# Positive and negative features of a head side by side: one pass for K^T V, 84-column matmuls for phi_q KV, and a new order

## The chip, the cores and the metric

The kernel runs on one core of one Trainium2 chip. TensorE (PE) multiplies matrices into PSUM; VectorE (DVE), ScalarE (ACT) and GpSimd (POOL) do the elementwise work and the sums; SyncE (SP) issues nearly all DMAs. The metric is the device time of one execution in microseconds. Before the change it is 297.68 us, the median of three runs from 297.18 to 297.76 us.

## The reference

One layer in bf16 with 2048 tokens of width D = 640: linear attention with learned feature maps on 32 heads of 20 dimensions, then a gated block without an activation function. Cut to what matters here:

```python
q, k, v = qkv of layernorm(x), heads of Dh = 20
pq = einsum("bhsd,hdf->bhsf", q, w_phi)          # and pk from k
phi_q = concat([softmax(pq), softmax(-pq)], -1)  # 40 features of a head
phi_k = concat([softmax(pk), softmax(-pk)], -1)
kv  = einsum("bhsf,bhsd->bhfd", phi_k, v)
z   = einsum("bhsf->bhf", phi_k)
num = einsum("bhqf,bhfd->bhqd", phi_q, kv)
den = einsum("bhqf,bhf->bhq", phi_q, z) + 1e-6
h   = x + (num / den) @ wo
out = h + ((ln(h) @ w_gate) * (ln(h) @ w_up)) @ w_down   # F = 1536
```

## The kernel before

Tokens are cut into NT = 16 tiles of P = 128 rows, D into NC = 5 chunks of 128. Features are 2 x 640 per token: the 640 positive ones of all heads (s = 0), then the 640 negative ones (s = 1). A chunk of 128 features of one sign touches 7 or 8 heads of 20 (the list CH, 36 heads over the five chunks).

Units, with the names that the order uses:

- `warm` is 48 matmuls on ones before data is there. `wk`, `x`, `y`, `wm`, `wv`, `c`, `wo` prepare weights (w_phi is multiplied into wq and wk; means are taken out). `s` computes layernorm's statistics of the rows; their inverse root goes into `rs` by a POOL instruction.
- `k`t (keys, L738): projection into PSUM, ten matmuls of 320 columns; then softexp (L725): DVE takes the largest absolute value (`mx`, L726) and multiplies it by `rs` (`nb`, L729, one column), ACT writes the two exponentials (L733). `K`t: DVE sums groups of 20 (L744) and takes reciprocals (L746), POOL multiplies all 1280 features by them in place (L747).
- `v`t: projection, ACT writes the values with a one behind each head's 20 (`vaug`, 21 columns a head, L753).
- `A`t and `B`t (kv_mm, L790): K^T V of a pair of tiles, for the positive (A) and the negative (B) features. A matmul has 128 features as weights and the 147 or 168 columns of the heads that they touch; each of A and B holds a PSUM buffer of two banks until `Aout` and `Bout` (kv_out, L812), where DVE multiplies by a mask (`Gkv`) that leaves only each feature's own head, and the epsilon is added to the column of sums. There are four such PSUM buffers (`PS`, pool p_ps) for everything.
- `q`t (queries, L758): projection and softexp as for keys, into one of three buffers `eq`; the positive half leaves at once by a DMA transpose into `phiqT`. `Q`t: DVE sums (L767), a ratio of the two sums of a head (L769, L770), POOL multiplies the negative half by it (L775), and a second DMA transpose takes that half.
- `n`t (num, L834): phi_q KV of a tile, twelve matmuls: two signs, five chunks, and the middle chunk in two parts since its heads lie in two PSUM banks. DVE divides (L862, L863), the result is transposed (on PE for the first two tiles, by DMA for the others).
- `h`t (watt): output projection, residual (L882), transpose into `hT`, statistics. `f`b.ft.j (fu): gate and up matmuls of a block of four tiles (in block 0 two tiles at a time), ACT copies the gate (L903), DVE multiplies (L905). `d`t and `e`t: down projection and the store.

Num of any tile needs K^T V of all sixteen. A block's `f` needs `h` of its tiles.

The order of every engine's queue is made by a planner in the kernel's text (`place`, L183) from the dictionary ORDER and the duration `t` and latency `lat` that each operation states. An engine's operations are sorted by the place of their unit in its list. At each step the planner looks at the first few of each queue that are left (AHEAD: 4 for PE and POOL, 6 for the others), takes of those whose inputs are already placed the one that can start first, and gives it its buffers; only if no engine has such an operation may it look further down the lists, and takes the first one that is ready. So a unit's place in the list is a preference, and what the queue becomes depends on the durations too. On the chip each engine runs its queue strictly in order and waits on semaphores.

Of the kernel before, what the change touches and what calls it, by code (L numbers as in the profile page):

```python
# [11 lines left out]
P = 128  # L12
# [17 lines left out]
NKV = 2 * sum(hi - lo + 1 for lo, hi in CH)  # L30

KVG = [[(0, 0), (1, 0), (2, 0)], [(3, 0), (4, 0)], [(0, 1), (1, 1), (2, 1)], [(3, 1), (4, 1)]]
# [28 lines left out]
    "DVE":  # L61
# [8 lines left out]
    "ACT":  # L70
# [8 lines left out]
    "POOL":  # L79
# [292 lines left out]
def _build(ctx, nc, A_x, A_wqkv, A_w_phi, A_wo, B_w_gate, B_w_up, B_w_down, out):  # L372
# [16 lines left out]
    phiqT = sb([P, 2, 2, NC, 512], BF16, "phiqT")  # L389
    KVsb = sb([P, E21 * NKV], BF16, "KVsb")  # L390
# [32 lines left out]
    phik = BK[:, :].rearrange("p (t s n) -> p t s n", t=NT, s=2)  # L423
    pq = phiqT[:, :, :, :, :].rearrange("p b s c n -> p (b s c n)")
# [30 lines left out]
    R_KV, R_Gkv = Reg(), regs(4)  # L455
# [87 lines left out]
    def act_sum(in_, func, acc, rd, wr):  # L543
        v = Buf(p_junk)
        g.op("ACT", lambda e: e.activation(out=junk[:, v.i, :], in_=in_, func=func, accum_out=acc),  # L545
             rd=rd, wr=wr, use=[v], t=0.93, lat=1.0)
# [16 lines left out]
    def stats(i0, n):  # L563
# [18 lines left out]
        g.op("DVE", lambda e: e.tensor_copy(sm[:, sl], PS[v.i][:, 1, 0:n]), rd=[v.R[1]], wr=R_sm[sl], use=[v], t=0.15, lat=0.2)  # L582
        if not act:
            v3 = Buf(p_t32)
            sq = lambda: t32[:, v3.i, 0:P * n].rearrange("p (t n) -> p t n", t=n)
            g.op("DVE", lambda e: e.tensor_tensor(out=sq(), in0=PS[v.i][:, 0, 0:P * n].rearrange("p (t n) -> p t n", t=n),
                                                  in1=ident[:, :].unsqueeze(1).to_broadcast([P, n, P]), op=ALU.mult),
                 rd=[v.R[0], R_id], wr=v3.R, use=[v, v3], t=0.09 + 0.15 * n, lat=0.2 + 0.15 * n)
            g.op("DVE", lambda e: e.tensor_reduce(out=sxx[:, sl], in_=sq(), axis=AX.X, op=ALU.add), rd=v3.R, wr=R_sxx[sl], use=[v3],
                 t=0.09 + 0.14 * n, lat=0.2 + 0.14 * n)  # L590
# [21 lines left out]
    def nmu_out(v, bk, w, eng):  # L612
        if eng == "ACT":
            g.op("ACT", lambda e: e.activation(out=nmu[:, w, :, :], in_=PS[v.i][:, bk, 0:NC].unsqueeze(2).to_broadcast([P, NC, P]),
                                               func=ACT.Copy, scale=-1.0 / SC), rd=[v.R[bk]], wr=[R_nmu[w]], use=[v], t=0.72, lat=0.8)
        else:
            g.op("DVE", lambda e: e.tensor_scalar(out=nmu[:, w, :, :], in0=PS[v.i][:, bk, 0:NC].unsqueeze(2).to_broadcast([P, NC, P]),  # L617
                                                  scalar1=-1.0 / SC, scalar2=None, op0=ALU.mult),
                 rd=[v.R[bk]], wr=[R_nmu[w]], use=[v], t=0.77, lat=0.85)
# [7 lines left out]
    def wk_in():  # L627
# [27 lines left out]
    def wp_round(w, i):  # L655
# [23 lines left out]
        if i % 2 == 0:  # L679
            g.op("ACT", lambda e: e.activation(out=dst, in_=PS[v.i][:, :, 0:HALF], func=ACT.Copy, scale=SC),  # L680
                 rd=v.R, wr=[R_Wp[w][i]], use=[v], t=0.62, lat=0.72)
        else:
            g.op("DVE", lambda e: e.tensor_scalar(out=dst, in0=PS[v.i][:, :, 0:HALF], scalar1=SC, scalar2=None, op0=ALU.mult),
                 rd=v.R, wr=[R_Wp[w][i]], use=[v], t=0.7, lat=0.8)
# [10 lines left out]
    def wv_centre(v, cs):  # L695
        for c in cs:
# [5 lines left out]
                 t=0.81, lat=0.9)  # L702


    def wo_mean(c):
# [4 lines left out]
             rd=[R_wsum[c]], app=[R_Wo[c]], t=0.2)  # L710
# [13 lines left out]

    def softexp(v, t, i, dst, regs_, use=()):  # L725
        g.op("DVE", lambda e: e.tensor_reduce(out=mx[:, i:i + 1], in_=PS[v.i][:, :, 0:HALF], axis=AX.XY, op=ALU.max,  # L726
                                              apply_absolute_value=True, negate=True), rd=v.R, wr=[R_mx[i]], use=[v],
             t=0.81, lat=0.9)
        g.op("DVE", lambda e: e.tensor_tensor(out=nb[:, i:i + 1], in0=mx[:, i:i + 1], in1=rs[:, t:t + 1], op=ALU.mult),  # L729
             rd=[R_mx[i], R_rs[t]], wr=[R_nb[i]], t=0.16, lat=0.2)  # L730
        for s in range(2):
            sc = rs if s == 0 else nrs
            g.op("ACT", lambda e, s=s, sc=sc: e.activation(  # L733
                out=dst(s).rearrange("p (b n) -> p b n", b=2), in_=PS[v.i][:, :, 0:HALF], func=ACT.Exp,
                bias=nb[:, i:i + 1], scale=sc[:, t:t + 1]), rd=v.R + [R_nb[i], R_rs[t], R_nrs[t]], wr=[regs_[s]], use=[v] + list(use),
                t=0.88, lat=0.96)

    def keys(t, after=()):  # L738
        U("k%d" % t)
        softexp(proj(t, 1, after), t, t, lambda s: phik[:, t, s, :], R_phik[t])  # L740
        U("K%d" % t)
        vs, vr = Buf(p_Ss), Buf(p_Rk)
        x = phik[:, t, :, :].rearrange("p s (h f) -> p (s h) f", f=DH)
        g.op("DVE", lambda e: e.tensor_reduce(out=Ssum[:, vs.i, :], in_=x, axis=AX.X, op=ALU.add), rd=R_phik[t], wr=vs.R, use=[vs],  # L744
             t=1.5, lat=1.52)
        g.op("DVE", lambda e: e.reciprocal(out=Rk[:, vr.i, :], in_=Ssum[:, vs.i, :]), rd=vs.R, wr=vr.R, use=[vs, vr], t=0.55, lat=0.62)  # L746
        g.op("POOL", lambda e: e.tensor_tensor(out=x, in0=x, in1=Rk[:, vr.i, :].unsqueeze(2).to_broadcast([P, 2 * H, DH]), op=ALU.mult),  # L747
             rd=vr.R + R_phik[t], wr=R_phik[t], use=[vr], t=2.36)

    def values(t):  # L750
# [5 lines left out]
             rd=v.R + [R_rs[t]], app=[R_vaug[t]], use=[v], t=0.8, lat=0.88)  # L756

    def queries(t, after=()):  # L758
# [8 lines left out]
        g.op("DVE", lambda e: e.tensor_reduce(out=Sq[:, vs.i, :], in_=eq[:, b.i, :, :].rearrange("p s (h f) -> p (s h) f", f=DH),  # L767
                                              axis=AX.X, op=ALU.add), rd=b.R, wr=vs.R, use=[b, vs], t=1.5, lat=1.52)
        g.op("DVE", lambda e: e.reciprocal(out=rq[:, vr.i, :], in_=Sq[:, vs.i, H:2 * H]), rd=vs.R, wr=vr.R, use=[vs, vr], t=0.38, lat=0.38)  # L769
# [222 lines left out]
    for t in range(0, NT, 2):  # L992
        kv_mm(0, t, t + 2)
# [53 lines left out]
```

## Time and profile before

| | |
|---|---|
| median of the runs (3) | 297.68 us |
| lowest, highest | 297.18, 297.76 us |
| span of the profiled execution, first to last instruction | 296.0 us |
| granted TensorE clock | 1.000 of full speed |
| matmuls; LDWEIGHTS | 2375; 2389 |
| K^T V matmuls of 147 and of 168 columns | 128 and 32 |
| num matmuls of 147 and of 84 columns | 128 and 64 |
| DVE `mx` x32, `nb` x32, mean of one | 810 ns, 386 ns |
| DVE sums of keys L744 x16, of queries L767 x16 | 1461 ns, 1476 ns |
| ACT exponentials, 640 elements, x64 | 883 ns |
| POOL L747 (keys) x16, L775 (queries) x16 | 2356 ns, 1269 ns |
| DMA transposes phiqT<-eq x32, issue to landing | 2.6 us |

The profile names an instruction by the line of the kernel that issues it; all matmuls in the main loops go through one helper, L552, and are told apart by what they write and read. Buffers share memory, so some names mislead: the gate's results are written into the space of `phik`, w_down into that of `vaug`. A matmul's duration holds its way through the array; the next one starts long before it ends.

### The profile page before, as it was taken

The numbers are of one execution on the slowest core, as the hardware profiler recorded it, in microseconds if no ns is written. First come the engines' busy times: TensorE is split into PE (matmuls) and PEld (weight loads), VectorE is DVE, ScalarE is ACT, GpSimd is POOL, SyncE is SP. The second block draws the span as 40 slices with busy tenths as digits, with TensorE's granted clock in tenths as the row PEclk, the third lists the DMA queues.
The fourth block names the chain that finished last, engine by engine and source line by source line (L and its number), as shares of the span: only waits on it lengthen the run. The fifth ranks groups of instructions, "written<-read, shape, count | busy, mean of one in ns | idle before, by whom it ended". The sixth has DMA issues, their size and how long they took to land.

```text
span 296.0 us, 5789 instructions
## 1 busy us (share of the span) xinstructions
PE 288.0 (97%) x2375; PEld 201.1 (68%) x2389; DVE 182.0 (61%) x314; ACT 136.3 (46%) x226; POOL 104.0 (35%) x140
## 2 busy tenths in 40 slices
PE   8999999999998999999999999999999999999996
PEld 8878767886876888878665666567645444654673
DVE  1799999999999888978768584431132224023122
ACT  1447878977747555615416323341343313332121
POOL 7428977869521332231500324123132000230010
PEclk9999999999999999999999999999999999999999
DMA  8998899301459543444622354331111000010012
GB/s 202 195 201 132 205 354 395 127 2 39 52 114 264 112 90 71 80 87 79 122 35 62 75 90 108 72 66 47 44 47 23 21 0 2 22 44 2 0 44 69
DMA packets 65194, 28.10 MB, mean 95 GB/s; under 512 B 55696, under 2 KB 63888, under 8 KB 65168
## 3 DMA queue, kind: packets, MB, share of 16 engines
q1 hardware_dynamic: 64240, 27.37, 40.8%
q10 hardware_dynamic: 928, 0.35, 0.5%
q8 instruction: 19, 0.31, 0.4%
q14 instruction: 7, 0.06, 0.1%
HBM read 11.82 MB, written 2.62 MB: 49 GB/s over the span
## 4 chain that ended last, share of the span: by engine, by line
PE 81%; DVE 14%; DMA 2%; issue 1%; ACT 1%; POOL 1%; POOLq 0%
PE ps L552 80%; DVE Ssum L744 4%; DVE mx L726 2%; DVE nb L729 2%; DVE Sq L767 2%; DMA phiqT<-eq 2%; DVE Rk L746 1%; ACT eq L733 1%; DVE ob L863 1%; PE ps L635 1%; POOL eq L775 0%; DVE rq L769 0%; DVE outb L946 0%; ACT phik L733 0%; DVE outb L617 0%
## 5 line engine op out<-in xcount | busy, mean ns | idle before, releaser
L552 PE MATMUL ps<-phik,Wgu 128*128 128x512 bf16 (+1 forms) x587 | 106.1, 336 | 0.7
L552 PEld LDWEIGHTS ps<-phik,Wgu 128*128 128x128 bf16 x600 | 58.3, 98 | 43.4
L552 PE MATMUL ps<-Wp,xT 128*128 128x320 bf16 x480 | 69.0, 299 | 0.6 <-ACT eq L733 0.6
L905 DVE TENSOR_TENSOR phik<-ps,gate 128x512 bf16<-128x512 f32 (+1 forms) x60 | 34.4, 582 | 55.6 <-PE ps L552 44.2
L552 PE MATMUL ps<-vaug,phik 128*128 128x320 bf16 (+4 forms) x543 | 65.5, 279 | 0.2
L903 ACT ACTIVATE gate<-ps 128x512 bf16<-128x512 f32 (+1 forms) x60 | 30.5, 511 | 67.1 <-PE ps L552 64.9
L552 PEld LDWEIGHTS ps<-vaug,phik 128*128 128x128 bf16 x544 | 48.1, 98 | 16.8 <-ACT phik L733 0.3
L552 PEld LDWEIGHTS ps<-Wp,xT 128*128 128x128 bf16 x480 | 46.1, 98 | 17.8 <-ACT eq L733 0.8
L921 POOL TENSOR_TENSOR outb<-t,x_all 128x640 bf16<-128x640 f32 x12 | 16.8, 1396 | 73.7 <-ACT t L918 71.9
L747 POOL TENSOR_TENSOR phik<-phik,Rk 128x1280 bf16<-128x1280 bf16 x16 | 37.4, 2356 | 9.2 <-DVE Rk L746 5.7
L775 POOL TENSOR_TENSOR eq<-eq,rq 128x640 bf16<-128x640 bf16 x16 | 20.3, 1269 | 35.0 <-DVE rq L770 31.0
L726 DVE TENSOR_REDUCE mx<-ps 128x1 f32<-128x640 f32 x32 | 25.9, 810 | 3.7 <-PE ps L552 3.5
L767 DVE TENSOR_REDUCE Sq<-eq 128x64 f32<-128x1280 bf16 x16 | 23.6, 1476 | 2.0 <-ACT eq L733 2.0
L918 ACT ACTIVATE t<-ps,mh,rs 128x640 f32<-128x640 f32 x12 | 10.6, 883 | 29.3 <-PE ps L552 21.4
L744 DVE TENSOR_REDUCE Ssum<-phik 128x64 f32<-128x1280 bf16 x16 | 23.4, 1461 | 0.0
L733 ACT ACTIVATE eq<-ps,nb,rs 128x640 bf16<-128x640 f32 x16 | 14.1, 883 | 16.7 <-DVE nb L729 16.6
L888 POOL TENSOR_SCALAR vpe<-shc 128x1 f32<-128x1 f32 x16 | 3.0, 191 | 51.2 <-ACT junk L545 50.9
L545 ACT ACTIVATE junk<-x_all 128x640 bf16<-128x640 bf16 x20 | 14.6, 735 | 10.0 <-DVE x_all L882 10.0
L733 ACT ACTIVATE phik<-ps,nb,rs 128x640 bf16<-128x640 f32 x16 | 14.1, 883 | 6.9 <-DVE nb L729 6.8
L753 ACT ACTIVATE vaug<-ps,rs 128x640 bf16<-128x640 f32 x16 | 12.6, 796 | 5.7 <-PE ps L552 5.7
L882 DVE SCALAR_TENSOR_TENSOR x_all<-ps,mh,x_all 128x640 bf16<-128x640 f32 x16 | 14.1, 884 | 0.8
L733 ACT ACTIVATE phik<-ps,nb,nrs 128x640 bf16<-128x640 f32 x16 | 14.1, 883 | 0.0
(77 smaller groups left out, 264.0 us busy)
## 6 DMA issues: line engine op xcount, KB each, us to landing
x_all<-in_A_x_dram SPq DMA_DIRECT2D x4, 640.0 KB, 10.9
out_dram<-outb SPq DMA_DIRECT2D x15, 160.0 KB, 1.8
Wgu<-in_B_w_gate_dram SPq DMA_DIRECT2D x1, 1920.0 KB, 12.1
Wgu<-in_B_w_up_dram SPq DMA_DIRECT2D x1, 1920.0 KB, 16.4
vaug<-in_B_w_down_dram SPq DMA_DIRECT2D x1, 1920.0 KB, 8.4
Wp<-in_A_wqkv_dram SPq DMA_DIRECT2D x1, 800.0 KB, 5.0
phiqT<-in_A_wqkv_dram SPq DMA_DIRECT2D x1, 800.0 KB, 5.2
Wo<-in_A_wo_dram SPq DMA_DIRECT2D x1, 800.0 KB, 7.2
```

The costliest lines, as they stand in the source:

```text
L545: g.op("ACT", lambda e: e.activation(out=junk[:, v.i, :], in_=in_, func=func, accum_out=acc), rd=rd, wr=wr, use=[v], t=0.93, lat=1.0)
L552: ins = e.matmul(o_, lhsT=l_, rhs=r_, start=s_, stop=p_, skip_group_check=True)
L726: g.op("DVE", lambda e: e.tensor_reduce(out=mx[:, i:i + 1], in_=PS[v.i][:, :, 0:HALF], axis=AX.XY, op=ALU.max, apply_absolute_value=True, ...
L733: g.op("ACT", lambda e, s=s, sc=sc: e.activation(out=dst(s).rearrange("p (b n) -> p b n", b=2), in_=PS[v.i][:, :, 0:HALF], func=ACT.Exp, b ...
L744: g.op("DVE", lambda e: e.tensor_reduce(out=Ssum[:, vs.i, :], in_=x, axis=AX.X, op=ALU.add), rd=R_phik[t], wr=vs.R, use=[vs], t=1.5, lat=1.52)
L747: g.op("POOL", lambda e: e.tensor_tensor(out=x, in0=x, in1=Rk[:, vr.i, :].unsqueeze(2).to_broadcast([P, 2 * H, DH]), op=ALU.mult), rd=vr.R ...
L767: g.op("DVE", lambda e: e.tensor_reduce(out=Sq[:, vs.i, :], in_=eq[:, b.i, :, :].rearrange("p s (h f) -> p (s h) f", f=DH), axis=AX.X, op= ...
L775: return e.tensor_tensor(out=x, in0=x, in1=rq[:, vr.i, :].unsqueeze(2).to_broadcast([P, H, DH]), op=ALU.mult)
L882: g.op("DVE", lambda e: e.scalar_tensor_tensor(out=xv, in0=PS[v.i][:, :, 0:HALF], scalar=mh[:, t:t + 1], in1=xv, op0=ALU.subtract, op1=ALU ...
L903: g.op("ACT", lambda e: e.activation(out=gate[:, vg.i, 0:P * n], in_=PS[v.i][:, 0, 0:P * n], func=ACT.Copy), rd=[v.R[0]], wr=vg.R, use=[v, ...
L905: g.op("DVE", lambda e: e.tensor_tensor(out=hhT[:, hb, ft, sl], in0=PS[v.i][:, 1, 0:P * n], in1=gate[:, vg.i, 0:P * n], op=ALU.mult), rd=[ ...
L921: g.op("POOL", lambda e: e.tensor_tensor(out=outb[:, vo.i, :], in0=t32[:, v3.i, :], in1=x_all[:, t, :], op=ALU.add), rd=v3.R + [R_h[t]], w ...
```

## The change

It puts the 20 positive and the 20 negative features of a head next to each other, so that a head's 40 features are one run and 128 features touch at most SL = 4 heads. There are then NQ = 10 chunks with 4 x 21 = 84 columns each, in K^T V and in num. The exponentials write into interleaved places; both halves of a query tile contain both signs, so both transposes come after POOL's multiplication. One K^T V accumulation takes the place of A and B. The mask is 5 x 4 (the pattern of the ten chunks repeats after five) and is made by three POOL instructions in place of ten DVE copies. The lists of ORDER are replaced whole, and the durations stated for the planner are changed nearly everywhere (a few are shown). AHEAD is as before.

```diff
-NKV = 2 * sum(hi - lo + 1 for lo, hi in CH)
-
-KVG = [[(0, 0), (1, 0), (2, 0)], [(3, 0), (4, 0)], [(0, 1), (1, 1), (2, 1)], [(3, 1), (4, 1)]]
+DF = 2 * DH
+NQ = 2 * NC
+HQ = [P * c // DF for c in range(NQ)]
+SL = 4
+KVW = SL * E21
...
     "PE":
-        "warm x3 wk s0 x0 x1 v0 k1 wm wv x2 x4 s2 k0 k3 k2 s4 v1 s8 k4 v5 k5 k8 v4 y1 k10 v11 v9 v6 v8 y3 k7 s12 v3 "
...
+        "s0 k1 wk x3 x1 wv x4 x0 q1 x2 k2 s2 k0 s4 k3 k5 k4 s8 v8 k7 A6 v1 k11 k8 wm v5 v3 v9 v10 k6 k14 s12 y1 v11 A4 "
...
-    phiqT = sb([P, 2, 2, NC, 512], BF16, "phiqT")
-    KVsb = sb([P, E21 * NKV], BF16, "KVsb")
+    phiqT = sb([P, 2, NQ, 512], BF16, "phiqT")
+    KVsb = sb([P, NQ * KVW], BF16, "KVsb")
...
+    pool_op(lambda e: e.memset(Gk[:, :, :], 1.0), 0.15, wr=[R_Gk])
+    affine(R_Gk, Gk[:, :, :], [[P - 3 * DF, NC], [-DF, SL]], 0, 1)
+    affine(R_Gk, Gk[:, :, :], [[3 * DF - P, NC], [DF, SL]], DF - 1, -1)
...
+    def signed(x, s):
+        return x.rearrange("p (b h s f) -> p b s h f", b=2, s=2, f=DH)[:, :, s, :, :]
+
     def softexp(v, t, i, dst, regs_, use=()):
...
-             t=0.81, lat=0.9)
+             t=0.735, lat=0.85)
         g.op("DVE", lambda e: e.tensor_tensor(out=nb[:, i:i + 1], in0=mx[:, i:i + 1], in1=rs[:, t:t + 1], op=ALU.mult),
-             rd=[R_mx[i], R_rs[t]], wr=[R_nb[i]], t=0.16, lat=0.2)
+             rd=[R_mx[i], R_rs[t]], wr=[R_nb[i]], t=0.1, lat=0.2)
         for s in range(2):
             sc = rs if s == 0 else nrs
             g.op("ACT", lambda e, s=s, sc=sc: e.activation(
-                out=dst(s).rearrange("p (b n) -> p b n", b=2), in_=PS[v.i][:, :, 0:HALF], func=ACT.Exp,
+                out=signed(dst(), s), in_=PS[v.i][:, :, 0:HALF].rearrange("p b (h f) -> p b h f", f=DH), func=ACT.Exp,
...
     def queries(t, after=()):
...
-        softexp(v, t, NT + t, lambda s: eq[:, b.i, s, :], b.R, [b])
+        softexp(v, t, NT + t, lambda: eq[:, b.i, :], b.R, [b])
         vs, vr = Buf(p_Sq), Buf(p_rq)
-        transpose(lambda: phiqT[:, bb, 0, :, P * tt:P * (tt + 1)], lambda: eq[:, b.i, 0, :], [b.R[0]], [R_phiqT[bb][0][tt]], [b])
...
         def f(e):
-            x = eq[:, b.i, 1, :].rearrange("p (h f) -> p h f", f=DH)
+            x = eq[:, b.i, :].rearrange("p (h s f) -> p s h f", s=2, f=DH)[:, 1, :, :]
             return e.tensor_tensor(out=x, in0=x, in1=rq[:, vr.i, :].unsqueeze(2).to_broadcast([P, H, DH]), op=ALU.mult)
...
-        transpose(lambda: phiqT[:, bb, 1, :, P * tt:P * (tt + 1)], lambda: eq[:, b.i, 1, :], [b.R[1]], [R_phiqT[bb][1][tt]], [b])
...
+            transpose(lambda k=k: phiqT[:, bb, NC * k:NC * (k + 1), P * tt:P * (tt + 1)], lambda k=k: eq[:, b.i, D * k:D * (k + 1)],
+                      b.R, [R_phiqT[bb][k][tt]], [b])
+
+    KVBUF = Buf(p_ps, 2)
+
+    def kv_mm(t0, t1):
+        U("A%d" % t0)
...
+                for c in range(NC * k, NC * (k + 1)):
+                    lo = HQ[c]
+                    col = KVW * (c - NC * k)
                     for t in range(t0, t1):
...
+                        o_ = (t * H + lo) * E21
+                        lst.append((PS[v.i][:, k, col:col + KVW], phik[:, t, P * c:P * (c + 1)], BV[:, o_:o_ + KVW], first, False))
...
+    def kv_out():
+        U("Aout")
...
+            g.op("DVE", lambda e, psv=psv, dst=dst: e.tensor_tensor(
+                out=dst[:, :, :, 0:DH], in0=psv()[:, :, :, 0:DH], in1=Gk[:, :, :].unsqueeze(3).to_broadcast([P, NC, SL, DH]), op=ALU.mult),
+                rd=[v.R[k], R_Gk], app=[R_KV], use=[v], t=0.5, lat=0.6)
+            g.op("DVE", lambda e, psv=psv, dst=dst: e.scalar_tensor_tensor(
+                out=dst[:, :, :, DH], in0=psv()[:, :, :, DH], scalar=0.5 * EPS_DEN, in1=Gk[:, :, :], op0=ALU.add, op1=ALU.mult),
...
     def num(t):
...
-            for s in range(2):
-                for c in range(NC):
...
+            for c in range(NQ):
+                bk = c // NC
+                col = E21 * (HQ[c] - HH2 * bk)
+                lst.append((PS[v.i][:, bk, col:col + KVW], phiqT[:, bb, c, P * tt:P * (tt + 1)], KVsb[:, KVW * c:KVW * (c + 1)],
+                            first[bk], False))
+                first[bk] = False
...
     for t in range(0, NT, 2):
-        kv_mm(0, t, t + 2)
-    kv_out(0)
-    for t in range(0, NT, 2):
-        kv_mm(1, t, t + 2)
-    kv_out(1)
+        kv_mm(t, t + 2)
+    kv_out()
```

More of the change, by code (lines that the diff above doesn't have):

```diff
@@ L393, in _build @@
     G = sb([P, NC, H], BF16, "G")
-    Gkv = sb([P, NKV], BF16, "Gkv")
+    Gk = sb([P, NC, SL], BF16, "Gk")
     ident = sb([P, P], BF16, "ident")
     ones = sb([P, P], BF16, "ones")
-    eq = sb([P, 3, 2, D], BF16, "eq")
+    eq = sb([P, 3, 2 * D], BF16, "eq")
     junk = sb([P, 2, D], BF16, "junk")
@@ L421, in _build @@
     rden = sb([P, 2, H], FP32, "rden")
-    phik = BK[:, :].rearrange("p (t s n) -> p t s n", t=NT, s=2)
-    pq = phiqT[:, :, :, :, :].rearrange("p b s c n -> p (b s c n)")
+    phik = BK[:, :].rearrange("p (t n) -> p t n", t=NT)
+    pq = phiqT[:, :, :, :].rearrange("p b c n -> p (b c n)")
     Wnat = pq[:, 0:NC * D].rearrange("p (a n) -> p a n", a=NC)
@@ L454, in _build @@
     R_const = Reg()
-    R_KV, R_Gkv = Reg(), regs(4)
+    R_KV, R_Gk = Reg(), Reg()
     R_phiqT = [[regs(4) for _ in range(2)] for _ in range(2)]
@@ L581, in stats @@
         sl = slice(i0, i0 + n)
-        g.op("DVE", lambda e: e.tensor_copy(sm[:, sl], PS[v.i][:, 1, 0:n]), rd=[v.R[1]], wr=R_sm[sl], use=[v], t=0.15, lat=0.2)
+        g.op("DVE", lambda e: e.tensor_copy(sm[:, sl], PS[v.i][:, 1, 0:n]), rd=[v.R[1]], wr=R_sm[sl], use=[v], t=0.08, lat=0.19)
         if not act:
@@ L769, in queries @@
-        g.op("DVE", lambda e: e.reciprocal(out=rq[:, vr.i, :], in_=Sq[:, vs.i, H:2 * H]), rd=vs.R, wr=vr.R, use=[vs, vr], t=0.38, lat=0.38)
-        g.op("DVE", lambda e: e.tensor_tensor(out=rq[:, vr.i, :], in0=Sq[:, vs.i, 0:H], in1=rq[:, vr.i, :], op=ALU.mult),
-             rd=vs.R + vr.R, wr=vr.R, use=[vs, vr], t=0.12, lat=0.2)
+        g.op("DVE", lambda e: e.tensor_reduce(out=Sq[:, vs.i, :], in_=eq[:, b.i, :].rearrange("p (g f) -> p g f", f=DH),
+                                              axis=AX.X, op=ALU.add), rd=b.R, wr=vs.R, use=[b, vs], t=1.4, lat=1.5)
@@ L773, in f, with sums @@
+        def sums(k):
+            return Sq[:, vs.i, :].rearrange("p (h s) -> p h s", s=2)[:, :, k]
+        g.op("DVE", lambda e: e.reciprocal(out=rq[:, vr.i, :], in_=sums(1)), rd=vs.R, wr=vr.R, use=[vs, vr], t=0.26, lat=0.38)
+        g.op("DVE", lambda e: e.tensor_tensor(out=rq[:, vr.i, :], in0=sums(0), in1=rq[:, vr.i, :], op=ALU.mult),
+             rd=vs.R + vr.R, wr=vr.R, use=[vs, vr], t=0.11, lat=0.2)
         def f(e):
-            x = eq[:, b.i, 1, :].rearrange("p (h f) -> p h f", f=DH)
+            x = eq[:, b.i, :].rearrange("p (h s f) -> p s h f", s=2, f=DH)[:, 1, :, :]
@@ L775, in f @@
             return e.tensor_tensor(out=x, in0=x, in1=rq[:, vr.i, :].unsqueeze(2).to_broadcast([P, H, DH]), op=ALU.mult)
-        g.op("POOL", f, rd=vr.R + [b.R[1]], wr=[b.R[1]], use=[b, vr], t=1.28)
-        transpose(lambda: phiqT[:, bb, 1, :, P * tt:P * (tt + 1)], lambda: eq[:, b.i, 1, :], [b.R[1]], [R_phiqT[bb][1][tt]], [b])
-    hof, KVO = 0, {}
-    for q_, grp in enumerate(KVG):
-        for c, s_ in grp:
-            lo, hi = CH[c]
-            KVO[c, s_] = E21 * hof
-            g.op("DVE", lambda e, c=c, lo=lo, hi=hi, hof=hof: e.tensor_copy(Gkv[:, hof:hof + hi - lo + 1], G[:, c, lo:hi + 1]),
-                 rd=[R_G[c]], app=[R_Gkv[q_]], t=0.1, lat=0.15)
-            hof += hi - lo + 1
@@ L797, in f @@
+    KVBUF = Buf(p_ps, 2)
+    def kv_mm(t0, t1):
+        U("A%d" % t0)
+        v = KVBUF
+        for k in range(2):
+            def f(e, k=k):
                 lst = []
                 first = t0 == 0
-                for c, s_ in grp:
-                    lo, hi = CH[c]
-                    col = KVO[c, s_] - KVO[grp[0]]
-                    n = E21 * (hi - lo + 1)
+                for c in range(NC * k, NC * (k + 1)):
+                    lo = HQ[c]
+                    col = KVW * (c - NC * k)
@@ L803, in f @@
                     for t in range(t0, t1):
-                        lst.append((PS[v.i][:, k, col:col + n], phik[:, t, s_, P * c:P * (c + 1)],
-                                    BV[:, t * H * E21 + E21 * lo:t * H * E21 + E21 * (hi + 1)], first, False))
+                        o_ = (t * H + lo) * E21
+                        lst.append((PS[v.i][:, k, col:col + KVW], phik[:, t, P * c:P * (c + 1)], BV[:, o_:o_ + KVW], first, False))
                         first = False
                 return mms(e, lst)
-            n = (t1 - t0) * len(grp)
+            n = (t1 - t0) * NC
@@ L809, in kv_mm @@
             g.op("PE", f, rd=[r for t in range(t0, t1) for r in R_phik[t]] + R_vaug[t0:t1], wr=[v.R[k]], use=[v],
-                 t=0.066 * n, lat=0.066 * n + 0.15)
-    def kv_out(j):
-        U("%sout" % "AB"[j])
-        v = KVBUF[j]
+                 t=0.041 * n, lat=0.041 * n + 0.15)
+    def kv_out():
+        U("Aout")
+        v = KVBUF
         for k in range(2):
-            grp = KVG[2 * j + k]
-            n = sum(CH[c][1] - CH[c][0] + 1 for c, s_ in grp)
-            o_ = KVO[grp[0]]
-            dst = KVsb[:, o_:o_ + E21 * n].rearrange("p (h e) -> p h e", e=E21)
-            mask = Gkv[:, o_ // E21:o_ // E21 + n].unsqueeze(2)
-            ncol = E21 if j else DH
-            def psv(k=k, n=n):
-                return PS[v.i][:, k, 0:E21 * n].rearrange("p (h e) -> p h e", e=E21)
-            g.op("DVE", lambda e, psv=psv, dst=dst, mask=mask, n=n, ncol=ncol: e.tensor_tensor(
-                out=dst[:, :, 0:ncol], in0=psv()[:, :, 0:ncol], in1=mask.to_broadcast([P, n, ncol]), op=ALU.mult),
-                rd=[v.R[k], R_Gkv[2 * j + k]], app=[R_KV], use=[v], t=0.15 + 0.00105 * n * ncol, lat=0.22 + 0.00105 * n * ncol)
-            if j == 0:
-                g.op("DVE", lambda e, psv=psv, dst=dst, mask=mask: e.scalar_tensor_tensor(
-                    out=dst[:, :, DH:E21], in0=psv()[:, :, DH:E21], scalar=EPS_DEN, in1=mask, op0=ALU.add, op1=ALU.mult),
-                    rd=[v.R[k], R_Gkv[k]], app=[R_KV], use=[v], t=0.19, lat=0.25)
@@ new lines, in kv_out, with psv @@
+            dst = KVsb[:, NC * KVW * k:NC * KVW * (k + 1)].rearrange("p (c h e) -> p c h e", c=NC, e=E21)
+            def psv(k=k):
+                return PS[v.i][:, k, 0:NC * KVW].rearrange("p (c h e) -> p c h e", c=NC, e=E21)
+            g.op("DVE", lambda e, psv=psv, dst=dst: e.tensor_tensor(
+                out=dst[:, :, :, 0:DH], in0=psv()[:, :, :, 0:DH], in1=Gk[:, :, :].unsqueeze(3).to_broadcast([P, NC, SL, DH]), op=ALU.mult),
+                rd=[v.R[k], R_Gk], app=[R_KV], use=[v], t=0.5, lat=0.6)
@@ L841, in f @@
             first = [True, True]
-            for s in range(2):
-                for c in range(NC):
-                    lo, hi = CH[c]
-                    for bk in range(2):
-                        l2, h2 = max(lo, HH2 * bk), min(hi, HH2 * bk + HH2 - 1)
-                        if l2 > h2:
-                            continue
-                        lst.append((PS[v.i][:, bk, E21 * (l2 - HH2 * bk):E21 * (h2 + 1 - HH2 * bk)],
-                                    phiqT[:, bb, s, c, P * tt:P * (tt + 1)],
-                                    KVsb[:, KVO[c, s] + E21 * (l2 - lo):KVO[c, s] + E21 * (h2 + 1 - lo)], first[bk], False))
-                        first[bk] = False
+            for c in range(NQ):
[4 more added lines that the diff above has]
+                first[bk] = False
             return mms(e, lst)
-        o_num = g.op("PE", f, rd=[R_KV, R_phiqT[bb][0][tt], R_phiqT[bb][1][tt]], wr=v.R, use=[v], t=0.68, lat=0.83)
+        o_num = g.op("PE", f, rd=[R_KV, R_phiqT[bb][0][tt], R_phiqT[bb][1][tt]], wr=v.R, use=[v], t=0.41, lat=0.56)
         vr, vo = Buf(p_rden), Buf(p_ob)
@@ L861, in rd_ @@
             return rden[:, vr.i, :].rearrange("p (b h) -> p b h", b=2)
-        g.op("DVE", lambda e: e.reciprocal(out=rd_(), in_=pv()[:, :, :, DH]), rd=v.R, wr=vr.R, use=[v, vr], t=0.38, lat=0.38)
+        g.op("DVE", lambda e: e.reciprocal(out=rd_(), in_=pv()[:, :, :, DH]), rd=v.R, wr=vr.R, use=[v, vr], t=0.27, lat=0.38)
         g.op("DVE", lambda e: e.tensor_tensor(
```

58 lines of the change are left out of this document (26 added, 32 removed), and 58 rows, old and new, of the table ORDER.

## The prediction

> **What bounds the kernel now.** I read the page first: busy shares, the slices, the chain that ended last.
>
> ```profile
> PE 288.0 (97%) x2375; PEld 201.1 (68%) x2389; DVE 182.0 (61%) x314; ACT 136.3 (46%) x226; POOL 104.0 (35%) x140
> ...
> PE   8999999999998999999999999999999999999996
> ...
> DVE  1799999999999888978768584431132224023122
> ...
> PE 81%; DVE 14%; DMA 2%; issue 1%; ACT 1%; POOL 1%; POOLq 0%
> ```
>
> TensorE is busy almost from end to end, and 81% of the chain is its own work. But the DVE row is full from the third slice to the thirteenth (slices of 7.4 us), and the chain's 14% of DVE must lie there. So next the busy times by stretch. I cut at the first matmul of num (85.5 us) and at the second num group after it (96.5 us, where the chain returns to PE for good).
>
> ```profile
> 8.30:56.00 47.70, 46.79 (x522) 36.23 (x520) 45.59 (x71) 34.86 (x51) 32.20 (x45) 1.00 0.98 243
> 56.00:85.50 29.50, 28.79 (x307) 23.51 (x304) 28.93 (x42) 21.82 (x36) 20.22 (x11) 1.00 0.20 31
> 85.50:96.50 11.00, 9.23 (x98) 7.17 (x98) 10.40 (x18) 7.31 (x14) 1.27 (x1) 1.00 1.06 241
> 96.50:293.00 196.50, 195.76 (x1356) 126.93 (x1370) 95.44 (x174) 70.98 (x127) 43.74 (x56) 1.00 0.26 56
> ```
>
> The columns after the stretch's length are PE, PEld, DVE, ACT and POOL busy, then the granted clock (1.00). From 96.5 us on only PE is full (195.76 of 196.50) and DVE is half idle: a microsecond of PE work saved there is a microsecond of time. From 8.3 to 85.5 us PE (75.6 of 77.2) and DVE (74.5) are both full: PE work saved there counts only if DVE also arrives earlier. Between them, the hand-over from keys to num, PE loses 1.77 us; what it waits for from 56 to 97 us:
>
> ```profile
> PE ps L477 <- DVE ob L863: 1.3, 2, 0.7
> PE ps L552 <- ACT eq L733: 0.6, 1, 0.6
> PE ps L552 <- DMA phiqT<-eq: 0.4, 1, 0.4
> ```
>
> Little to gain from order alone: these 2.3 us, and about as much again in small waits elsewhere.
>
> **The price of a narrow matmul.** The change replaces 147- and 168-column matmuls by 84-column ones, each with a 128x128 weight load as before, so I need the step from one matmul's start to the next, not its duration (228 and 202 ns, mostly pipeline). The timeline of PE has a pure run of each kind of work, K^T V and then num:
>
> ```profile
> 80.69 3.03 PE L552 MATMUL ps<-vaug,phik 128*128 128x147 bf16 x43
> ...
> 85.51 2.25 PE L552 MATMUL ps<-KVsb,phiqT 128*128 128x147 bf16 x36
> ```
>
> K^T V: 42 steps in 3.03 - 0.23 (the last matmul's own duration) = 2.80 us, 66.7 ns. Num mixes widths: a tile is eight of 147 and four of 84 columns, so three tiles have 35 steps in 2.02 us, 23 of them wide: (2.02 - 23 x 0.0667) / 12 = 40.5 ns for 84 columns. There they come in pairs between wide ones; would a long run hold that pace? The chain of waits shows the start, where weight blocks change at every matmul:
>
> ```profile
> 7.52 0.10 PE ps L552 x5
> 7.62 0.30 PE ps L635 x5
> ```
>
> Five one-column matmuls with five full weight loads take 0.10 us, so loads alone do not forbid 40 ns. I take 40.5 ns; the bounds are 20 ns a step (these five) and 66.7 ns (no gain from width).
>
> A rule of the Trainium skill speaks against this: "TensorE: Matmul & The Clock Gate", section "Back-to-back issue gap", gives about 81 ns for each load-and-matmul pair at 128 columns in a real kernel. The runs above are faster at 147 columns, so the trace disagrees; by 81 ns for all old and new ones only num's 32 fewer matmuls would be saved, 2.6 us.
>
> **The change part by part, from the profiled execution's 296.0 us.** The runs' median is 297.68, so 1.68 us lie around the span; I add them at the end.
>
> 1. Num, on the path, PE-bound stretch. A tile falls from 8 x 66.7 + 4 x 40.5 = 696 ns to 10 x 40.5 = 405 ns; 16 tiles save 4.65 us. Bounds by the steps above: 16 x (696 - 667) = 0.5 to 16 x (696 - 200) = 7.9.
> 2. K^T V. Ten matmuls a tile as before, 667 to 405 ns, 16 tiles: 4.2 us. It lies from 57 to 84 us, beside a full DVE. What can DVE drop before num? Its slots there (from one start to the next) include q2 and q3, which num of the first two tiles does not need: two maxima and their nb at 0.77 + 0.45 us and one Sq group of 2.1, so 4.5 us can move behind; and the mask step below. So DVE can arrive some 5 us earlier, but only if the new order does this; I take 3.2 of the 4.2, bounds 0 and 4.2. One thing helps: K^T V held two of the four PSUM buffers, now one, and PE's wait of 0.6 us for ACT's exponential at 73 us is a wait for a buffer.
> 3. The mask step, six DVE instructions to four.
>
> ```profile
> L825 DVE TENSOR_TENSOR KVsb<-ps,Gkv x4: 435/530/625, 83.3 to 85.0; 128x440 bf16<-128x440 f32 x1, 128x280 bf16<-128x280 f32 x1, 128x462 bf16<-128x462 f32 x1, 128x294 bf16<-128x294 f32 x1
> L829 DVE SCALAR_TENSOR_TENSOR KVsb<-ps,Gkv x2: 205/224/242, 83.9 to 84.4; 128x22 bf16<-128x22 f32 x1, 128x14 bf16<-128x14 f32 x1
> ```
>
> Two of 400 elements at about 0.58 and two small ones for 2.12 + 0.45: 0.96 us less DVE, part of the 5 us of step 2; nothing more is counted. The ten Gkv copies (1.4 us of DVE before 8.3 us, when it waits for the first weights) go at nothing, and three small POOL instructions come, 0.2 us each by the G ones: they precede the Phi ones, which wait 1.0 us for a DMA. Without that cover they cost 0.6.
> 4. Exponentials write runs of 20 with gaps. The nearest row is the values' eviction (L753), which writes 20 of each 21: 796 ns for 640 elements against 883 for the exponential. I take nothing; ACT is 73 and 74% busy in the two full stretches, and the 40 exponentials there would add 4 us to 57 of 77 if each lost 0.1 us: still cover. The POOL multiplication of the queries goes over gaps; 1.27 us now, 2.36 at most (the full-width keys row): POOL is idle enough, and the price is latency to num.
> 5. The query transposes. Both now wait for that POOL instruction; before, the first left after the exponential. SP issues one in 1.2 us, so phi_q of a tile is complete up to 1.2 us later, and behind it in SP's queue wait the transposes of o and h and the stores. eq has three buffers and was held until the second transpose anyway. From 96.5 us on later tiles hide it; at the hand-over it may show once: 0 to 1.2, I take 0.3.
> 6. The order, all engines and queues, with new durations in the planner. Its bounds: PE's waits of some 4 us gone (-4), or new ones. For those the row to read is nb, a one-column product for which the planner's figure falls from 0.16 to 0.10 us:
>
> ```profile
> L729 DVE TENSOR_TENSOR nb<-mx,rs x32: 90/160/2123, 17.9 to 164.8; 128x1 f32<-128x1 f32 x32
> ...
> 38.30 2.12 DVE L729 TENSOR_TENSOR nb<-mx,rs 128x1 f32<-128x1 f32 x1
> ...
> 35.74 4.67 POOL L747 TENSOR_TENSOR phik<-phik,Rk 128x1280 bf16<-128x1280 bf16 x2 [0.21 <-DVE Rk L746]
> ```
>
> The 2.12 us one began while POOL multiplied keys and ended with it (40.42 and 40.41 us). The 20 of them before 85.5 us took 8.9 us of DVE slots where 0.1 each would be 2.0: a plan with 0.1 is 6.9 us short in the stretch without slack. Against it, the maxima were planned at 0.81 and step every 0.73-0.77, so the old plan had reserves that the new one lacks. Bounds -4 to +6.9; I take 0.
>
> The Trainium skill, "SBUF — State Buffer", section "Who interferes with whom", says that a DVE instruction with two SBUF inputs blocks against a GpSimd one that reads SBUF; nb is one, and these rows agree. By that rule the stalls stay after the change, which is the slower rival's ground.
>
> Sum: 296.0 - 4.65 - 3.2 + 0.3 = 288.45, plus 1.68: **290.1 us**.
>
> **Rivals.**
> - DVE sets the date of num. All of K^T V's gain turns into PE waits between 56 and 85 us and num starts at 85.5 as before; only num's gain is left: 297.68 - 4.65 = 293.0. For it: DVE 98% busy there; against it, 4.5 us of query work that can move.
> - The order also closes the gaps of the hand-over and the small ones: 290.1 - 1.0 (rest of K^T V) - 4 = 285. For it: PE then has q projections to put in, and a PSUM buffer more; against: the chain num, o, h, hT to the first gate matmul has a DMA of 4.97 us and two DVE steps that no order shortens.
> - Slower: the stalls of nb come on top. PE's queue is in order, and each projection or K^T V group that waits for a late DVE holds the ready work behind it. If nothing of K^T V is gained and all 6.9 us arrive at num, it starts at 92.4, and the time is 297.68 - 4.65 + 6.9 = 299.9. It decides from a num later than 85.5 + 4.65 = 90.2 us. For it: DVE has no slack and the durations shrank; against: the old order met the same stalls, and PE has work for such waits.
> - The change does not pay: 84 columns in long runs cost 66.7 ns. Then 297.68 - 0.5 = 297.2. Against it: both runs above. (By the 81 ns of the Trainium skill's matmul page it would be 295.1.)
>
> **How the numbers follow.** Chances: forecast 0.60 (287.5 to 292), DVE date 0.15 (292 to 296), closed gaps 0.12 (283 to 287.5), slower 0.10, no gain from width 0.03. A range of 284.5 to 296 leaves out the slower case and the ends, no more than 2 in 10. Runs of this kernel spread 0.58 us, so 0.2% (0.6 us) is what can be told from no change: faster than 297.1 has 0.87, within it 0.03, slower 0.10.
>
> **What would show it.** PE's mean step of the K^T V and num runs at 40 ns, 32 fewer matmuls; PE busy about 280 us; num's first matmul at 81 to 83 us, and 96.5 us to the end shorter by about 4 us. Exponentials still 0.88 us. I am wrong if the 84-column run steps at over 50 ns, if PE's waits before 100 us pass 6 us, or if SP's queue holds h transposes behind a query's so that gate matmuls wait.

## The result, and the profile after

The changed kernel takes 298.62 us (median of 18 runs, 298.06 to 300.07) against 297.28 us for the kernel before, run beside it (18 runs, 296.39 to 298.19): a ratio of 1.0049, 95% interval 1.0036 to 1.0063. It is slower by about half a per cent, where 290.1 us and a range of 284.5 to 296.0 had been forecast. The profiled execution spans 296.9 us, against 296.0 before. The page of the changed kernel, with the same lines as shown of before:

```profile
PE 282.0 (95%) x2346; PEld 192.5 (65%) x2357; DVE 185.7 (63%) x302; ACT 136.8 (46%) x226; POOL 104.6 (35%) x143
...
PE   8999999787967999999999999999999999999996
...
DVE  0799999999997989988775657352213232323201
...
PE 72%; DVE 21%; issue 3%; DMA 1%; POOL 1%; SPq 0%; ACT 0%; DVEq 0%; ACTq 0%; POOLq 0%
```

PE's busy time fell by 6 us, and the span did not follow: DVE's share of the chain rose from 14 to 21%, and PE's row has values of 6 to 8 in five of the six slices from the eighth to the thirteenth (52 to 96 us), where before only the thirteenth was not a nine. The busy times of the same kernel by stretch, cut at num's first matmul and at the point where PE is full for good (columns as before: length, then PE, PEld, DVE, ACT, POOL busy, granted clock, DMA):

```profile
8.30:56.00 47.70, 45.65 (x504) 34.65 (x501) 45.89 (x71) 34.56 (x51) 32.64 (x47) 1.00 0.99 239
56.00:93.10 37.10, 29.86 (x336) 22.44 (x336) 35.76 (x45) 24.84 (x41) 21.23 (x11) 0.95 0.18 32
93.10:103.50 10.40, 9.15 (x105) 7.03 (x106) 9.09 (x19) 6.52 (x11) 0.49 (x2) 1.00 0.51 133
103.50:293.00 189.50, 188.92 (x1297) 120.34 (x1307) 93.95 (x167) 69.64 (x124) 43.07 (x56) 1.00 0.30 63
```

Num starts at 93.1 us instead of 85.5. From there to the end it takes 203.8 us instead of 210.5: 6.7 us won behind num, 7.6 lost ahead of it. In the second stretch PE is idle for 7.2 of 37.1 us and DVE for 1.3. The timeline of PE there:

```profile
83.40 2.45 PE L553 MATMUL ps<-vaug,phik 128*128 128x84 bf16 x60
88.09 2.59 PE L553 MATMUL ps<-vaug,phik 128*128 128x84 bf16 x40 [2.24 <-POOL phik L751]
90.47 2.28 PE L553 MATMUL ps<-Wp,xT 128*128 128x320 bf16 x10
93.14 0.95 PE L553 MATMUL ps<-KVsb,phiqT 128*128 128x84 bf16 x20 [0.39 <-DVE KVsb L820]
```

The reader is to see two things. Sixty 84-column matmuls in a run take 2.45 us: (2.45 - 0.20) / 59 = 38 ns a step, so the narrow matmuls keep what was forecast. And PE waits 2.24 us for POOL's multiplication of the last keys; the forty matmuls behind that wait take as long as the sixty ahead of it, at a granted clock of 0.61 (88.09 to 90.47 us); e5 and e8 take this up.

What DVE did meanwhile: its instruction nb, the one-column product of two SBUF columns, in the view of that tile, and two places of DVE's timeline with the POOL instructions that ran there.

```profile
L733 DVE TENSOR_TENSOR nb<-mx,rs x32: 90/159/2053, 18.2 to 178.6; 128x1 f32<-128x1 f32 x32
```

```profile
53.59 1.74 DVE L733 TENSOR_TENSOR nb<-mx,rs 128x1 f32<-128x1 f32 x1
...
56.50 1.73 DVE L733 TENSOR_TENSOR nb<-mx,rs 128x1 f32<-128x1 f32 x1
```

```profile
52.96 2.35 POOL L751 TENSOR_TENSOR phik<-phik,Rk 128x1280 bf16<-128x1280 bf16 x1 [0.56 <-DVE Rk L750]
55.87 2.35 POOL L751 TENSOR_TENSOR phik<-phik,Rk 128x1280 bf16<-128x1280 bf16 x1 [0.56 <-DVE Rk L750]
```

Each nb that starts while POOL multiplies keys lasts until POOL is done (53.59 + 1.74 = 55.33 and 52.96 + 2.35 = 55.31; 58.23 and 58.22). In both kernels every nb longer than 0.3 us, 18 in all, ends 14 to 18 ns behind the end of a POOL multiplication: 16 of them of keys, two, in the kernel before, of queries. The 21 nb ahead of num take 13.8 us of DVE's slots, from one start to the next; before, 20 took 8.9.

### The profile page after: what moved, and what is told of

Read it like the earlier page. It is cut to its first block, busy times and chain, and to the rows that moved or that the text cites. A ratio compares the mean times of both kernels' runs of the same rounds, so it can differ in the third digit from the quotient of the medians.

```text
span 296.9 us, 5723 instructions
## 1 busy us (share of the span) xinstructions
PE 282.0 (95%) x2346; PEld 192.5 (65%) x2357; DVE 185.7 (63%) x302; ACT 136.8 (46%) x226; POOL 104.6 (35%) x143
## 4 chain that ended last, share of the span: by engine, by line
PE 72%; DVE 21%; issue 3%; DMA 1%; POOL 1%; SPq 0%; ACT 0%; DVEq 0%; ACTq 0%; POOLq 0%
PE ps L553 71%; DVE Ssum L748 6%; DVE mx L730 4%; DVE nb L733 3%; DVE Rk L750 2%; DVE Sq L770 1%; DMA phiqT<-eq 1%; DVE rq L776 1%; PE ps L636 1%; DVE ob L849 1%; DVE Wp L684 0%; POOL eq L781 0%; DVE sxx L590 0%; DVE t L587 0%; SPq L462 0%
## 5 line engine op out<-in xcount | busy, mean ns | idle before, releaser
L553 PE MATMUL ps<-Wp,xT 128*128 128x320 bf16 x480 | 69.9, 301 | 3.8 <-ACT eq L737 2.3
L553 PE MATMUL ps<-vaug,phik 128*128 128x320 bf16 (+3 forms) x543 | 60.6, 273 | 2.3 <-POOL phik L751 2.2
L553 PEld LDWEIGHTS ps<-vaug,phik 128*128 128x128 bf16 x544 | 44.3, 100 | 18.2 <-POOL phik L751 2.4
L737 ACT ACTIVATE eq<-ps,nb,rs 128x640 bf16<-128x640 f32 x16 | 14.1, 882 | 10.7 <-DVE nb L733 10.4
L733 DVE TENSOR_TENSOR nb<-mx,rs 128x1 f32<-128x1 f32 x32 | 15.5, 489 | 0.9 <-POOL rs L600 0.5
L865 DVE TENSOR_TENSOR mh<-ps,mv 128x1 f32<-128x1 f32 x16 | 2.5, 155 | 19.0 <-PE ps L553 18.9
```

The source lines that it names most:

```text
L553: ins = e.matmul(o_, lhsT=l_, rhs=r_, start=s_, stop=p_, skip_group_check=True)
L737: g.op("ACT", lambda e, s=s, sc=sc: e.activation(out=signed(dst(), s), in_=PS[v.i][:, :, 0:HALF].rearrange("p b (h f) -> p b h f", f=DH), ...
```

## The experiments

Two theories stood against each other, with a third beside them: the stalls of nb carry the loss (theory 1); the order itself does, since it puts the queries' sums ahead of the last key's (rival 2); or the new layout costs something (rival 3 in e3 and e4; in e1, rival 3 is that nb waits for something else).

**e1: nb without its second SBUF input.** The queues stay as they are, and the traces show the same order on PE, DVE, ACT and POOL; the inverse root comes in as the scalar operand of the instruction.

```diff
-        g.op("DVE", lambda e: e.tensor_tensor(out=nb[:, i:i + 1], in0=mx[:, i:i + 1], in1=rs[:, t:t + 1], op=ALU.mult),
+        g.op("DVE", lambda e: e.tensor_scalar(out=nb[:, i:i + 1], in0=mx[:, i:i + 1], scalar1=rs[:, t:t + 1], scalar2=None, op0=ALU.mult),
```

> The changed kernel, with nb as a tensor_scalar instruction (mx from SBUF, the inverse root as its scalar operand) in place of a tensor_tensor with two SBUF inputs; every queue stays as it is. Theory 1 (stalls): the new order fails because nb waits for POOL's running keys multiplication (21 nb before num take 13.8 us of DVE slots where 0.1 us each is 2.1), so DVE brings num late (first num matmul at 93.1 us). Without the second input nb's mean falls from 489 ns to about 150, num starts at 82 to 86 us and the time is 287 to 291. Rival 2 (order): the queries' sums stand before the last key's sum on DVE and cost their 5 to 8 us with or without stalls: num still after 90 us, 295 to 298. Rival 3 (nb waits for something else, such as the inverse root): its mean stays near 490 ns and the time near 298.5.

Measured: 287.43 us, ratio to the kernel before 0.9661 (0.9642 to 0.9680); 11.2 us less than the changed kernel. nb in e1, and the stretches of e1:

```profile
L733 DVE TENSOR_SCALAR nb<-mx,rs x32: 114/205/215, 17.6 to 167.9; 128x1 f32<-128x1 f32 x32
```

```profile
56.00:82.40 26.40, 24.68 (x304) 19.35 (x301) 25.03 (x39) 20.00 (x34) 19.02 (x10) 1.00 0.22 39
82.40:92.80 10.40, 9.16 (x105) 7.04 (x106) 9.17 (x19) 6.53 (x11) 0.50 (x2) 1.00 0.52 137
92.80:282.00 189.20, 188.62 (x1297) 120.35 (x1307) 94.30 (x167) 69.74 (x124) 42.94 (x56) 1.00 0.29 63
```

The longest nb falls from 2053 to 215 ns, though the usual one is a little slower (205 against 159 ns). The 21 ahead of num take 3.5 us of slots instead of 13.8. Num starts at 82.4 us, 10.7 us earlier; behind it nothing changes (203.6 us to the end against 203.8). Eleven nb of e1 start while POOL multiplies keys, and they last 114 to 215 ns too. So with the same queues the loss is in nb's stalls, as theory 1 had it. Rival 2 falls for this kernel: the order with the queries' sums first costs little once DVE does not stall (PE still waits 1.28 us for the last key). That nb waits for the inverse root falls too, since it reads it in e1 as well; and so does the layout as the cause, since e1 has it.

**e2: the same edit in the kernel before.**

> The kernel before with the same edit of nb alone. Theory 1: there the queue was planned with longer DVE figures that already held the stalls, and num (85.5 us) came 4 us before PE's work allowed no more, so little is won: nb's mean falls from 386 to about 150 ns, the time by 0 to 2 us, 295.3 to 297.3. A rival says that the stalls cost the kernel before just as much: 290 to 292.

Measured: 294.23 us, ratio 0.9894 (0.9878 to 0.9911), 3.4 us less and so more than expected. nb's slots ahead of num fall by 4.4 us (8.9 to 4.5), num starts at 83.7 us, 1.8 us earlier, and PE's waits of 0.6 us for ACT and for the o of one tile go. So the old queue hid only a part of its stalls, where nearly all had been expected. With nb mended in both, the change is worth 294.23 - 287.43 = 6.8 us.

**e3 and e4: layout and queues exchanged.** The planner is given every queue operation by operation, with no freedom:

```diff
-    AHEAD = {"PE": 4, "DVE": 6, "ACT": 6, "POOL": 4, "SP": 6}
+    AHEAD = {"PE": 1, "DVE": 1, "ACT": 1, "POOL": 1, "SP": 1}
...
-        for o in ops:
-            self.rank.setdefault((o.eng, o.unit), len(self.rank))
-        queue = {e: sorted((o for o in ops if o.eng == e), key=lambda o: (self.rank[e, o.unit], o.n)) for e in self.ENGS}
+        nth, name = {}, {}
+        for o in sorted(ops, key=lambda o: o.n):
+            k = nth.get((o.eng, o.unit), 0)
+            nth[o.eng, o.unit] = k + 1
+            name[o] = "%s:%d" % (o.unit, k)
+        queue = {e: sorted((o for o in ops if o.eng == e), key=lambda o: self.rank[e, name[o]]) for e in self.ENGS}
```

> The new layout, with every engine's queue written out as it was in the kernel before (K^T V of the negative features and its mask left out, both transposes of a query tile where the second one was). Theory 1: the layout pays by itself: num's 4.65 us, less what the later first transposes cost around num of the first tiles (two more transposes to wait for, 1.2 us each, on PE at 83 to 90 us, and again at tiles 8, 9 and 15): 292 to 298. Rival 3 (the layout costs something itself, in strided writes or in 84-column runs): over 298, with exponentials longer than 0.88 us or steps over 50 ns.

Measured: 302.35 us, ratio 1.0160 (1.0142 to 1.0179), a miss on the upper side. Num starts at 85.4 us, when it did before: the 4 us that PE saves on K^T V are idle time, as in the rival in which DVE sets num's date. The four longest rows of PE's waits in e3:

```profile
PE ps L591 <- DMA phiqT<-eq: 2.4, 2, 1.9
PE ps L591 <- issue: 2.0, 1, 2.0
PE ps L591 <- DMA phik<-ob: 2.0, 1, 2.0
PE ps L591 <- DVE KVsb L858: 1.8, 1, 1.8
```

The query transposes, now both behind POOL's multiplication, and the transposes of o behind them are waited for, at num of the first tiles and again at 139 and 177 us. On top, the mean granted clock of this execution is 0.983, where it was 1.000: 5.1 of 300.9 us, lost behind such waits (0.73 from 85.4 to 98.0 us). The time lies where rival 3 had it, over 298, but its marks are absent: exponentials take 0.88 us, and 20 K^T V matmuls of 84 columns 0.94 us, 39 ns a step. The layout needs queues of its own.

> The layout of before, with every queue written out as it is in the changed kernel (each negative K^T V group behind the positive one, its mask behind the other mask, the first transpose of a query tile where the first of the two was). Theory 1: this order carries the loss: the changed kernel's 298.6 plus num's 4.65 and most of K^T V's 4.2, since 5 groups of K^T V follow the last key: 303 to 309. Rival 3: the layout carries the loss, and this is at or below 298.

Measured: 304.9 us, ratio 1.0253 (1.0231 to 1.0276), as expected. Num starts at 94.7 us, with 13.8 us of nb's slots ahead of it. Under the new queues the layout is worth 304.9 - 298.6 = 6.3 us by the medians; the profiled executions show 5.5 of them, 3.9 behind num (207.7 us from its start to the end, against 203.8) and 1.5 ahead of it.

**e5: the last key's sum first**, with nb as in the changed kernel, the queues written out as in e3. DVE's queue around the move (on POOL the last key's multiplication moves with it, ahead of those of queries 2 and 0):

```diff
-K9:1 Q1:0 k15:0 Q1:1 k15:1 Q1:2 Q2:0 Q2:1 Q2:2 Q0:0 Q0:1 Q0:2 K15:0 K15:1
+K9:1 Q1:0 k15:0 Q1:1 k15:1 Q1:2 Q2:0 Q2:1 K15:0 K15:1 Q2:2 Q0:0 Q0:1 Q0:2
```

> The changed kernel with its queues written out and one move: the last key's sum and reciprocal stand on DVE ahead of the ratio of query 2 and the sums of query 0 (they stood behind both), and on POOL its multiplication ahead of those of queries 2 and 0. nb stays a tensor_tensor. Theory 1 (stalls carry the loss): the last K^T V group comes some 2 us earlier, but num needs the queries just as much, and the stalls of nb are all still there: 296 to 299. Rival 2 (order carries it): num of the first tile within 3 us of the kernel before's 85.5 us, 290 to 293.

Measured: 297.41 us, ratio 0.9978 (0.9948 to 1.0008), and ten runs that fall into two groups: three at 295.0, whose mean granted clock is 1.000, and seven from 297.1 to 298.3, with 0.994 or less. Num starts at 90.3 us in the profiled one, 2.9 us earlier than in the changed kernel, and the span is 296.6 us all the same. Rival 2 falls: 90.3 us is not within 3 us of 85.5, and even the three runs at 295.0 are over its 293. Nor are the 2.9 us a price of the order alone, since the move met fewer stalls: nb's slots ahead of num take 12.5 us instead of 13.8, and the longest ratio of the query sums there 0.62 instead of 1.90 us. But where did the 2.9 us go? The stretches of e5:

```profile
90.20:93.00 2.80, 1.85 (x27) 1.75 (x28) 1.57 (x4) 0.62 (x2) 0.18 (x1) 0.68 0.52 117
93.00:105.00 12.00, 11.82 (x95) 8.42 (x94) 9.45 (x17) 7.71 (x13) 1.91 (x3) 0.79 0.63 192
```

PE is busy but at a granted clock of 0.68 and 0.79 (the number behind POOL's); these are averages, for the trace has 0.50 from 91.2 to 98.0 us and 1.00 around it. PE had just waited 1.9 us for the K^T V mask and then 0.85 us for a query's transpose. The missing share is 0.32 x 2.8 + 0.21 x 12.0 = 3.4 us.

**e8: that wait filled**, with matmuls on ones whose result num overwrites.

```diff
+        v = Buf(p_ps, 2)
+        if t == 1:
+            U("fill")
+            g.op("PE", lambda e: mms(e, [(PS[v.i][:, 0, 0:P], ones[:, :], ones[:, :], True, True) for _ in range(34)]),
+                 rd=[R_one], wr=v.R, use=[v], t=1.9, lat=2.05)
         U("n%d" % t)
-        v = Buf(p_ps, 2)
```

> The kernel of e5 (297.4 us) with 34 matmuls on ones before the first num, into num's own PSUM buffer before num overwrites it: 1.9 us of work without use where PE waited 2.1 us for the K^T V mask. Theory: e5 brought num 2.9 us earlier and won nothing, since after that wait the granted clock was 0.68 and then 0.79 for the next 15 us, about 3 us of PE's work; with the wait filled the clock stays at 1.00 and the time is 293.5 to 295.5. Rival: the low clock hides behind DVE there and e5's gain went elsewhere (the queries that were put back); then the time stays at 297 to 298.

Measured: 295.76 us, ratio 0.9952 (0.9938 to 0.9967), all runs from 295.3 to 296.4; the median lies 0.3 us above the expected range. The two stretches in e8:

```profile
90.20:93.00 2.80, 1.51 (x31) 1.22 (x28) 2.29 (x5) 0.90 (x3) 0.00 (x0) 1.00 0.62 137
93.00:105.00 12.00, 11.87 (x109) 9.26 (x110) 10.45 (x23) 8.01 (x14) 3.46 (x6) 1.00 0.92 211
```

The clock is 1.00 and the same 12 us hold 109 matmuls instead of 95. Useless work made e5 faster, and the upper group of runs is gone: that the lost clock took e5's gain is shown. The changed kernel has the same fault: behind its wait of 2.24 us its granted clock was 0.50, from 88.6 to 92.0 us. Ahead of num that cost little by its trace: K^T V ended at 90.7 us, but DVE, still at the sums of a query, reached the mask at 91.8. Its twelve runs with this clock (a mean of 0.994, as profiled, or 0.993) take 298.1 to 298.7 us; six others, in which the mean clock is lower still (0.988), 299.4 to 300.1.

**e6: queues arranged with the stalls counted.** nb stays a tensor_tensor; operations were moved within the queues, and nb and the ratio of the query sums were counted as lasting until the end of a POOL multiplication that they meet.

> The new layout with nb as a tensor_tensor, and queues that were arranged anew with nb and the ratio of the query sums counted as waiting for the end of the POOL multiplication that they meet. Theory 1: the stalls can be arranged around (nb where POOL is idle): nb's sum before num falls from 13.8 us to under 8, num at 84 to 87 us, the time 288 to 293. A rival says that with 16 keys multiplications of 2.36 us on POOL the stalls are met anyhow in a queue this full: 295 to 299.

Measured: 289.09 us, ratio 0.9721 (0.9700 to 0.9741). nb in e6:

```profile
L771 DVE TENSOR_TENSOR nb<-mx,rs x32: 95/158/611, 18.3 to 169.2; 128x1 f32<-128x1 f32 x32
```

The same instructions stand where POOL is idle; the longest is 0.61 us, the 21 ahead of num take 3.3 us of slots, and num starts at 84.2 us. Other waits changed with the queues, so not all of the 9.5 us against the changed kernel is nb's.

**e7: e1 with queues of its own.** The same rearrangement, with nb as a tensor_scalar.

> The changed kernel with nb as a tensor_scalar (as in e1, 287.4) and queues arranged anew for it, only the ratio of the query sums counted as waiting for POOL. What PE still loses in e1 is 1.3 us before the last K^T V group and 2.2 us at the hand-over to num. Theory 1: these are waits of the order, and most of the 2.2 us stay since num, division, transposes and the output projection follow each other there: 285.5 to 287. A rival says that the order as planned is already the best: 287 to 288.5.

Measured: 285.89 us, ratio 0.9615 (0.9594 to 0.9637). Num starts at 80.4 us; the two longest of PE's waits that are left in e7:

```profile
PE ps L513 <- DVE ob L887: 1.2, 2, 0.9
PE ps L591 <- POOL ones L550: 1.0, 1, 1.0
```

The first is the division at the hand-over, 1.3 us before the change and 1.2 us in e1, the second the start of the kernel. This version is 3.9% faster than the kernel before and 4.3% faster than the changed one.

## Why the prediction was wrong, point by point

- **The narrow matmul** (step 1): right. 38 ns a step against 40.5 forecast, in long runs too, so the rival that width does not pay is out, and the 81 ns of the Trainium skill's page "TensorE: Matmul & The Clock Gate", section "Back-to-back issue gap", do not hold here. Behind num 3.9 us were won under the same queues (e4) where 4.65 had been forecast. The bound of 20 ns a step was a misreading: successive starts of those one-column matmuls lie 25 ns apart.
- **K^T V** (step 2): mis-sized. I took 3.2 of 4.2 us on the condition that the new order moves queries behind num. It did the opposite: four sums of queries stand ahead of num instead of three, and the last key's sum moved from 76.1 to 83.5 us. 1.5 us were left (e4), and under the old queues nothing (e3).
- **The mask, the strided exponentials, POOL over gaps** (steps 3 and 4): right. Two masks of 0.57 and two of 0.24 us, exponentials at 0.88, POOL at 1.27 us as before.
- **The transposes** (step 5): 0.3 us forecast. In the changed kernel's profile PE does not wait for them; with the old queues (e3) PE waits 4.4 us for transposes of queries and of o, besides the clock that falls there. The price belongs to a layout whose queues are not remade, and I had counted one hand-over only.
- **The order** (step 6): the step that failed. I took 0 between -4 and +6.9. It cost 11.2 us (e1 against the changed kernel): nb's slots ahead of num are 10.3 us longer, and num starts 10.7 us later. The sign that the prediction had named came: PE's waits before 100 us are 11.5 us, where 6 were the limit. Without the stalls (e1) num starts at 82.4 us, inside the forecast 81 to 83; that e1's time is below the forecast 290.1 is partly luck for the other terms, since e1 also lacks the stalls that the old kernel had (3.4 us in e2). Two errors lie in the step. I had the row and the mechanism, and set against it that the other durations had been generous. But just that reserve was what the change removed: the figures of the maxima and sums came down to the measured ones while nb's went to 0.10 us, so the plan had less reserve and kept the stalls. (No run changes the durations without the lists, so what each of them did to the order stays open.) And the bound was taken from the stalls that the old order met (20 nb, 6.9 us above 0.1 each), as if they were a property of the instruction. They are one of the order: what an nb costs depends on where it meets POOL, from 0.09 to 2.05 us, and a new order can meet more of them: 21 nb, 13.8 - 2.1 = 11.7 us.
- **The slower rival** named the mechanism, the place and the result: num at 92.4 us and 299.9 us, against 93.1 and 298.6. That its numbers are so close is partly luck: its 6.9 us are the stalls that the old order already had, while the new one added 4.9 us of nb's slots (8.9 to 13.8) and other work of DVE ahead of num, and 6.7 us were won behind num where it counted 4.65. Its chance of 0.10 was too small for a stretch that the text itself called without slack. The Trainium skill's page "SBUF — State Buffer", section "Who interferes with whom", says that a DVE instruction with at most one SBUF input, outside the perf modes that use both ports, does not contend with GpSimd; e1 agrees, with 215 ns at most, if its scalar operand is not counted as such an input.
- **The closed gaps**: against this rival the text set a DMA of 4.97 us between num and the first gate matmul. That DMA is a transpose of queries that a later tile's num waits for (0.4 us), so it was no argument on that chain; e7's queues won another 1.5 us against e1.

## What to carry to other kernels

When a change brings a new order made from stated durations, compare these with measured slots, instruction by instruction, above all on an engine without slack; one figure that leaves out a wait of 0.5 us on average, 21 times, cost here more than the change could win. Rows whose longest is over ten times their median (90/159/2053) point at such an instruction: look at what else ended when it ended, and change its operands (e1) or place it where the other engine is idle (e6). A saving on one of two full engines was worth nothing while the other one's list stayed as long (e3).

## What the runs showed of the hardware

- A one-column DVE product of two SBUF columns that starts while POOL multiplies keys (2.35 us) lasts until that is done, and ends 14 to 18 ns behind it. With one of the columns as scalar operand no such wait is seen (114 to 215 ns, eleven of the 32 started within such a multiplication). The edit changes the kind of the instruction together with its operand, and no run tells the two apart. The ratio of the query sums, also two SBUF inputs, shows the same wait, up to 1.90 us, and ends 46 to 51 ns behind POOL.
- Behind some waits of PE of 1.9 to 2.2 us the granted clock fell to 0.50: in the changed kernel for 3.4 us (wait of 2.24 us), in e5 for 6.8 us (1.92 us, then 0.85), in e3 for 6.8 us around 88 to 95 us (1.84, 0.55 and 2.01 us) and for 3.4 us at 180 us (1.96 us). It did not fall behind 1.86 us in e3 (at 139 us), in three of e5's ten runs, nor behind any single wait of 1.4 us or less that stands alone, such as e1's 1.28. In e5 it shows in the time: two groups of runs some 2.5 us apart, one group when the wait was filled. The Trainium skill's page "TensorE: Matmul & The Clock Gate", section "Why this matters for your kernels", warns of idle gaps above some 3 us; here shorter ones sufficed.
